# Loads on two queues, half-partition decay loads and a new hand-written order in a fused linear-attention and long-convolution kernel

## The chip, the cores and the metric

The kernel runs on one core of one Trainium2 chip. Its time is the device time in microseconds (us) of one execution. Three runs of the kernel before gave a median of 153.95 us, from 152.64 to 155.37.

The core has engines that run their own instruction streams in order and meet through semaphores: PE (TensorE, matrix products into the banks of PSUM), DVE (VectorE), ACT (ScalarE), POOL (GpSimd) and SP (SyncE). Transfers between DRAM and the on-chip memory are issued by an instruction on the queue of some engine and carried out by 16 DMA engines.

## The reference

Two stages follow one another. The first is a recurrence over 768 positions for 4 batches and 8 heads of width 48 (`state` is 48 x 48 per head); the second is a gated long convolution over the 384 channels that the first gives:

```python
for t in range(S):                       # S = 768
    cur = einsum('bhd,bhe->bhde', u * k[t], v[t])
    y[t] = einsum('bhd,bhde->bhe', r[t], state + cur)
    state = w[t] * state + einsum('bhd,bhe->bhde', k[t], v[t])
x = y.transpose(0, 2, 1, 3).reshape(B, S, 384)
x1, x2, x3 = split(x @ w_proj, 3)        # w_proj: 384 x 1152
conv = irfft(rfft(x2, axis=1) * rfft(filter_fft, axis=0))
out = (x1 * conv * x3) @ w_out
```

r, k, v and w are float32 of shape 4 x 8 x 768 x 48; the output is 4 x 768 x 384 float32.

## The kernel before

**Chunks.** Each batch is cut into 6 chunks of 128 positions, 24 chunks in all. Chunk i needs four loads, `lw{i}`, `lk{i}`, `lr{i}`, `lv{i}`, each 128 positions x 8 heads x 48 float32 = 192 KB. A head's row of one position is 48 x 4 = 192 bytes, and it is the longest run that is contiguous on both sides. Chunks 0 and 1 form groups of their own; the others go in pairs, so there are 13 groups `gi`, and some operations (`ln`, `vb`, `rk`, `ru`, `rh`, `cc`, `vc`) treat a whole group.

**First stage, for one chunk.** `ln` (ACT, line 1319) takes the logarithm of w. `cs` (PE, lines 1345 to 1350) forms running sums of it over the 128 positions by two products with triangular masks, and four products with a column of ones for the total. `ex` (ACT, 1353) is the exponential of the sums in place in PSUM. `kq` (DVE, 1356) multiplies it with k and r. `ph` (ACT, 1360) gives the chunk's total decay. `tr` (PE, 1368) transposes kq in eight 128 x 128 blocks into a bank, and `qk` (DVE or ACT) copies the bank out. `sc` (PE, 1380) is the score product, `mt` copies it out with its causal mask on DVE (`D` one half, `M` both), or copies it plainly on ACT (`A`, `N`) and `mc` on POOL cuts the triangle. `kv` and `ki` (PE) form the next state, `su` (DVE, 1431) scales it. `rk`, `ru`, `rh` and `cc` give the weight of the term with u, `vc` multiplies it with v, and `xa`, `yi` or the addition in `xn` brings it into the result. `ys` and `y` (PE, 1450 and 1458) form the output, `xn` evicts it, `yt` (PE, 1482) transposes it and `xT` copies it out of the bank as the input of the second stage.

**Second stage, for one batch b.** `p`/`cp` is the projection x1 and its eviction, `q`/`cq` (DVE, 1649) x3 times x1, `xw`/`cxw` the projection x2, `sd` sums and differences of its two halves, `f`/`cf` the forward transform, `u` and `p{b}.{n}` on DVE the product with the filter's spectrum, `E`/`cE`/`aE` (and `dE` for the folded form, letter `Q`) the inverse transform, `yE` the gate, `o`/`co`/`so` the output projection, its eviction and the store. The second stage of batch b runs between the chunks of batch b+1; that of batch 3 stands alone at the end.

**What sets the order.** A string, `ORDER`, names every operation, the engine that does it, the PSUM bank where it takes one, and sometimes an operation that it must follow. A line reads for example `cs0 P 4`, `kq0 D`, `lw0 S` or `rh0 G kq0`. Each engine works through its own lines in the order of the string; `-` means that the operation is left out because another form does it. Semaphores for the data are added by the framework. `warm n b` puts n products of 256 columns of zeros on PE. All 96 loads, the load of u and of the filter and all 13 stores are on SP's queue; the four weight loads are on POOL's.

**Buffers.** There are 3 slots for w (`NLW`), 4 for k and r and for v (`NLD`), each holding a pair of chunks; 3 groups of the products (`NG`); 4 of `kq` and `qk` (`NF`); 5 output slots (`NO`), taken in turn by `co`. An instruction that fills a slot waits for the last reader of it.

Of the kernel before, what the change touches and what calls it, by code (L numbers as in the profile page):

```python
# [9 lines left out]
FP32 = mybir.dt.float32  # L10
# [28 lines left out]
NLW, NLD, NG, NF, NS, NX, NO = 3, 4, 3, 4, 3, 3, 5  # L39
# [5 lines left out]
warm 16 0  # L45
pads D
smalls D
zeros D
lw0 S
first A  # L50
ln0 A
imaps G
maske G smalls
maps G smalls
ang2 D
ang1 D
lw3 S
lw2 S
lr0 S
lk0 S  # L60
kz2 G
maskn G
cs0 P 4
kz0 G
ln2 A
u S
signs D
maski G
ia1.0 G
ex0 A  # L70
kq0 D
ia2.0 D
warm 9 1
cs3 P 6
kz3 G zeros
cs2 P 2
ur A
warm 5 1
um P 0
rk0 G  # L80
ub A
lv0 S
lw1 S
lr3 S
lk1 S
tr0 P 1
qk0 D
ph0 A
vb0 A
ex3 A  # L90
ln1 A
ang0 D
ru0 G ia2.0
rh0 G kq0
cc0 D
kz1 D
vc0 D
warm 6 0
sc0 P 0
warm 2 4  # L100
cs1 P 4
mt0.1 -
mt0.0 N
kv0 P 0
ex2 A
ex1 A
ia0.0 G zeros
su0 D
mc0.0 C cc0
lk3 S  # L110
lr1 S
mc0.1 -
warm 4 1
yi0 P 0
kq3 D
y0 P
xn0 A
tr3 P 1
kq1 D
lk2 S  # L120
lr2 S
lv1 S
lw4 S
lw5 S
tr1 P 0
rk1 G
ru1 D
rh1 G ru1
ph1 A
qk3 D  # L130
xa0 -
ph3 A
kq2 D
lv2 S
lv3 S
yt0 P 6
sc3 P 4
xT0 A
mt3.0 M
qk1 A  # L140
vb1 A
ph2 A
warm 4 7
tr2 P 6
lr4 S
lk4 S
ki1 P 1
sc1 P 2
qk2 A
mc3.0 -  # L150
mt1.1 -
kv1 P
warm 2 7
sc2 P 6
cc1 D
rk2 G
lk5 S
ru2 D
ia2.1 G
vc1 G  # L160
mc1.1 -
mt1.0 M
mc1.0 -
mt2.1 -
mt3.1 -
lr5 S
ln3 A
warm 5 0
cs4 P 4
yi1 P 2  # L170
rh2 G ru2
su1 D
vb2 G ru2
ys1 P
mc2.1 -
lv5 S
lv4 S
cc2 D
vc2 G cc2
mt2.0 M  # L180
wproj1 G mt2.0
ki2 P 0
y1 P
lw6 S
warm 5 1
kv2 P
xn1 A
ex4 A
cs5 P 2
xa1 -  # L190
mc2.0 -
yt1 P 1
su2 D
ki3 P 0
kv3 P
# [3 lines left out]
mc3.1 -  # L199
xT1 A  # L200
kq4 D
tr4 P 1
ex5 A
ph4 A
wproj0 G su2
kq5 D
su3 D
xn2 A
yi3 P 4
ys3 P  # L210
qk4 A
y3 P
rk3 G
xn3 D
warm 4 6
tr5 P 6
qk5 D
xa2 -
ph5 A
yt2 P 2  # L220
lw7 S
xa3 -
yt3 P 7
xT3 D
xT2 D
ki4 P 5
warm 4 1
sc5 P 6
trig A
sin0 A  # L230
sin2 A
vb3 G xn3
mt5.1 -
mc5.1 -
ia1.1 G xT2
kv4 P
sc4 P 3
ia0.1 G xT2
mt4.0 N
ru3 D  # L240
rh3 D
cc3 D
vc3 G cc3
warm 7 1
xw0.2 P 0
is A
mt5.0 M
su4 D
mt4.1 -
xw0.0 P 2  # L250
mc5.0 -
mc4.0 C
yi5 P 6
cxw0.2 D
yi4 P 4
cxw0.0 D
lk7 S
sin1 A
table A
ln4 A  # L260
lr7 S
mc4.1 -
ys5 P
ys4 P
y5 P
xn5 D
y4 P
xn4 D
p0.0.0 P 0
lk6 S  # L270
xa4 -
xa5 -
yt5 P 6
p0.2.0 P 3
lr6 S
rk4 G xn5
xT5 D
yt4 P 2
cs7 P 6
cp0.0.0 D  # L280
filt S
cp0.2.0 D
cs6 P 4
xT4 A
xw0.4 P 0
ex7 A
kq7 D
lv7 S
ex6 A
kq6 D  # L290
cxw0.4 A
if3 A
p0.0.1 P 2
tr7 P 1
ph7 A
cp0.0.1 A
tr6 P 6
qk6 A
qk7 A
sd0.0.0 D  # L300
ru4 D
lw8 S
lw9 S
p0.2.1 P 0
ph6 A
warm 4 7
f0.0 P 2
lv6 S
cp0.2.1 A
cf0.0 A  # L310
sd0.1.0 D
f0.2 P 5
sc7 P 0
mt7.1 -
rh4 D
fsd0 D
fsd1 D
lk8 S
lr9 S
cf0.2 A  # L320
warm 5 7
sc6 P 6
lr8 S
mt7.0 N
mt6.1 -
warm 6 4
h1 P 1
mt6.0 M
ln5 A
cc4 D  # L330
h2 P 4
mc6.0 -
mc7.1 -
lk9 S
mc7.0 C rh4
hc1 A
hg1 D
vb4 G
vc4 G fsd1
lv8 S  # L340
lv9 S
mc6.1 -
lk11 S
hc2 A
h0 P 6
hg2 D
kv6 P 3
su6 D
lk10 S
lw10 S  # L350
lr10 S
hc0 A
cs8 P 0
wproj2 G
warm 2 2
yi6 P 4
y6 P
lw11 S
hg0 D
ex8 A  # L360
xn6 A
xa6 -
yi7 P 2
ys7 P
y7 P
xn7 A
xa7 -
cs9 P 4
kq8 D
lr11 S  # L370
ex9 A
yt6 P 3
yt7 P 7
xT7 D
kq9 D
xT6 A
ki7 P 2
kv7 P
tr8 P 6
qk8 D  # L380
ph8 A
rk5 G cc4
ru5 G
vb5 A
lv11 S
xw1.0 P 0
lr12 S
lv10 S
tr9 P 3
sc8 P 6  # L390
if2 A
ph9 A
lw12 S
rh5 D
cc5 D
lk12 S
lw13 S
lv13 S
cxw1.0 A
qk9 A  # L400
lv12 S
mt8.1 -
su7 D
lk13 S
mt8.0 M
vc5 G cc5
lk15 S
f0.1 P 4
q0.2.0 P 3
ki8 P 2  # L410
cq0.2.0 D
mc8.1 -
sc9 P 0
lr13 S
cf0.1 A
mt9.0 N
mc9.0 C
if1 A
kv8 P
q0.0.1 P 6  # L420
q0.2.1 P 3
yi8 P 4
ln6 A
u10.0 D
mt9.1 -
su8 D
cq0.0.1 D
mc8.0 -
u00.0 D
yi9 P 1  # L430
lw15 S
ys9 P
ys8 P
y8 P
lk14 S
mc9.1 -
xn8 A
lw14 S
lr14 S
xa8 -  # L440
y9 P
lr15 S
q0.0.0 P 6
lv15 S
yt8 P 0
cs10 P 4
if0 A
xn9 A
xa9 -
ki9 P 2  # L450
yt9 P 1
lk17 S
cq0.0.0 D
lv14 S
xT8 A
ex10 A
xT9 A
kv9 P
lw17 S
cs11 P 6  # L460
ex11 A
p1.2.0 P 0
cq0.2.1 D
rk6 G cq0.0.1
cp1.2.0 A
su9 D
lv17 S
ru6 D
xw1.2 P 1
kq10 D  # L470
tr10 P 3
kq11 D
rh6 G ru6
ph10 A
cxw1.2 A
p1.0.0 P 4
cc6 D
p0.0 D
ph11 A
qk10 A  # L480
cp1.0.0 A
ln7 A
tr11 P 7
vb6 G
vc6 G
q1.0.0 P 1
qk11 D
sc10 P 3
sc11 P 6
q1.2.0 P 5  # L490
lr17 S
lw16 S
ki10 P 0
mt10.1 A
cq1.0.0 D
cs12 P 1
mt10.0 D
lk16 S
yi10 - 3
ys10 P  # L500
mt11.1 -
mc11.1 -
mc10.0 -
mc10.1 G
y10 P
mt11.0 N
cs13 P 6
kv10 P
cq1.2.0 D
ex12 A  # L510
xn10 V
kq12 D
vb7 G
ex13 A
E0.0 P 4
mc11.0 C mt10.0
ph12 A
yi11 - 1
cE0.0 A
su10 D  # L520
kq13 D
ph13 A
tr12 P 3
ys11 P
kv12 P 0
aE0.0.0 D
rk7 G
ru7 G
xa10 -
qk12 A  # L530
y11 P
E0.1 P 6
xn11 V
xa11 -
su12 D
cE0.1 A
aE0.0.1 D
dE0.0.0 -
rh7 G aE0.0.0
yt11 P 1  # L540
xT11 D
yt10 P 0
ki13 P 3
tr13 P 2
E0.2 P 4
kv13 P
aE0.1.1 D
aE0.1.0 D
xT10 A
qk13 D  # L550
ln8 A
cE0.2 A
sc12 P 6
lk18 S
lr16 S
mt12.1 -
su13 D
aE0.2.1 D
aE0.2.0 D
mt12.0 N  # L560
sc13 P 0
p1.0.1 P 2
mt13.1 D
mt13.0 D
lv16 S
cp1.0.1 A
cs14 P 6
ex14 A
dE0.1.0 -
xw1.4 P 4  # L570
q1.0.1 P 1
cc7 D
kq14 D
cq1.0.1 D
p1.2.1 P 3
vb8 A
cxw1.4 A
rk8 G
ru8 G
rh8 G aE0.1.0  # L580
tr14 P 0
ph14 A
mc12.1 -
cp1.2.1 A
dE0.1.1 -
sd1.1.0 D
q1.2.1 P 5
cs15 P 3
ki14 P 2
kv14 P  # L590
qk14 A
ex15 A
vc7 G sd1.1.0
sd1.0.0 D
sc14 P 6
mt14.0 A
ln9 A
su14 D
mt14.1 D
mc14.1 -  # L600
f1.0 P 0
lw18 S
f1.2 P 6
cf1.0 A
dE0.0.1 -
kq15 D
cq1.2.1 D
ph15 A
dE0.2.1 -
mc12.0 C cq1.0.1  # L610
cf1.2 A
tr15 P 2
cc8 D
cs16 P 0
yi12 - 4
y12 P
yE0.0 D
vc8 G
qk15 D
mc13.1 -  # L620
f1.1 P 6
yi13 P 2
xn12 V
sc15 P 4
xa12 -
ex16 A
kq16 D
mc13.0 -
ys13 P
y13 P  # L630
cf1.1 A
ph16 A
tr16 P 7
mt15.1 D
vb9 A
cs17 P 0
xn13 A
lw19 S
mt15.0 D
mc14.0 G yE0.0  # L640
ex17 A
qk16 D
yE0.1 G
lk19 S
ki15 P 6
kv15 P
yi14 - 3
ys14 P
lr18 S
lv18 S  # L650
yt12 P 5
xa13 -
su15 D
yt13 P 2
xT12 A
y14 P
xn14 X
mc15.1 -
ki16 P 7
kv16 P  # L660
sc16 P 5
lv19 S
lr19 S
ln10 A
rk9 G mt15.1
xT13 D
kq17 D
mc15.0 -
ph17 A
mt16.1 A  # L670
dE0.2.0 -
xa14 G
xw2.0 P 3
mt16.0 D
yi15 P 0
ys15 P
y15 P
su16 D
cxw2.0 A
u11.0 D  # L680
cs18 P 6
yt14 P 2
xn15 A
xT14 D
ex18 A
xa15 -
lr20 S
lw21 S
cs19 P 4
ex19 A  # L690
tr17 P 3
yt15 P 0
wout G su16
xT15 A
kq18 D
rk10 G
ph18 A
kq19 D
ru9 D
qk17 A  # L700
lw20 S
ph19 A
p2.0.0 P 1
tr18 P 0
ru10 D
xw2.2 P 6
mc16.0 -
q2.0.0 P 4
rh9 D
rh10 D  # L710
cp2.0.0 A
cxw2.2 A
lk20 S
yE0.2 D
tr19 P 2
cq2.0.0 D
sc17 P 6
vb10 G rh10
p2.2.0 P 1
cc9 D  # L720
mt17.1 -
o0.0 P 4
mt17.0 M
qk18 A
cc10 D
qk19 A
mc17.1 -
lk21 S
q2.2.0 P 0
lr21 S  # L730
cp2.2.0 A
ln11 A
kv18 P 3
co0.0 A
mc16.1 G
cq2.2.0 D
sc18 P 1
mt18.1 D
# [1140 lines left out]
```

## Time and profile before

| what | value |
|---|---|
| median of 3 runs | 153.95 us (152.64 to 155.37) |
| the profiled execution's own time | 153.79 us |
| its span, first to last instruction | 152.1 us |
| busy: PE, DVE, ACT, POOL | 142.4, 135.6, 123.1, 96.1 us |
| instructions: PE, DVE, ACT, POOL | 1725, 252, 204, 101 |
| moved by DMA | 26.23 MB in 104118 packets, 100129 of them under 512 bytes |
| loads: issue to landing, median | 3.8 to 4.4 us |

The span is 1.69 us below the time of the same execution; what lies around the span is not seen in the profile. "Idle" of an engine is time in which none of its instructions runs; the view of waits says what ended it. Neighbouring instructions of DVE and ACT overlap a little, so that the mean durations of all 252 DVE instructions add up to about 151.3 us against 135.6 us busy, which is 0.062 us of overlap for each. Instructions that issue DMAs are not counted as busy; they stand as `SPq` on SP's queue.

### The profile page before, as it was taken

How to read it: one execution, taken by the hardware profiler on the slowest of the kernel's cores; microseconds unless marked ns; L12 is line 12 of the kernel's file. 1: busy time of each engine (PE TensorE's matmuls, PEld its weight loads, DVE VectorE, ACT ScalarE, POOL GpSimd, SP SyncE). 2: the span in 40 equal slices, each digit the busy share in tenths (PEclk: the TensorE clock that was granted, in tenths of full speed). 3: DMA queues.
4: the chain of work that ended last, by engine and by line, in shares of the span. 5: the costliest groups of instructions: out<-in, count | busy, mean ns of one | idle time of the engine just before them, and what ended most of it. 6: DMA issues, size and time to landing. Idle time of an engine off the chain costs nothing.

```text
span 152.1 us, 4409 instructions
## 1 busy us (share of the span) xinstructions
PE 142.4 (94%) x1725; PEld 95.3 (63%) x1725; DVE 135.6 (89%) x252; ACT 123.1 (81%) x204; POOL 96.1 (63%) x101
## 2 busy tenths in 40 slices
PE   7986999999999999999999999999999999999980
PEld 5654667666556657567666776576687666656530
DVE  3589996989969999999989999999999999999950
ACT  4576849989979989997889899979999987576370
POOL 6577989944069567888968974885299164830310
PEclk9999999999999999999999999999999999999999
DMA  4999899999999999989899899998940000002956
GB/s 97 216 214 223 163 221 174 203 182 272 250 209 170 197 172 219 212 162 218 170 203 218 160 203 192 198 213 169 324 133 0 4 0 0 4 0 88 395 210 240
DMA packets 104118, 26.23 MB, mean 172 GB/s; under 512 B 100129, under 2 KB 102690, under 8 KB 104098
## 3 DMA queue, kind: packets, MB, share of 16 engines
q1 hardware_dynamic: 102498, 24.78, 74.2%
q0 software_dynamic: 1600, 1.18, 5.6%
q8 instruction: 13, 0.21, 0.5%
q14 instruction: 7, 0.06, 0.1%
HBM read 22.41 MB, written 4.72 MB: 178 GB/s over the span
## 4 chain that ended last, share of the span: by engine, by line
PE 42%; DVE 15%; DMA 13%; SPq 10%; ACT 8%; issue 5%; POOL 4%; POOLq 1%; DVEq 0%; ACTq 0%
SPq L1313 10%; PE banks L1624 7%; PE banks L1511 6%; PE banks L1780 5%; DMA w<-in_w_dram 5%; PE banks L1661 3%; PE banks L1368 3%; PE banks L1380 3%; DMA v<-in_v_dram 3%; DMA kr<-in_r_dram 3%; DVE kq L1356 3%; PE banks L1458 3%; DMA kr<-in_k_dram 2%; ACT banks L1353 2%; PE banks L1716 2%
## 5 line engine op out<-in xcount | busy, mean ns | idle before, releaser
L1209 POOL TENSOR_TENSOR rk<-kr 128x768 bf16<-128x768 f32 (+1 forms) x13 | 23.0, 1766 | 9.5 <-DMA kr<-in_r_dram 5.9
L1624 PE MATMUL banks<-xT,wproj 128*128 128x384 bf16 x144 | 27.9, 326 | 0.2 <-ACT x L1213 0.2
L1356 DVE TENSOR_TENSOR kq<-banks,kr 128x768 bf16<-128x768 f32 x24 | 22.4, 949 | 3.6 <-DMA kr<-in_k_dram 1.7
L1401 POOL TENSOR_SCALAR_AFFINE_SELECT mt<-mt 128x512 bf16<-128x512 bf16 (+1 forms) x15 | 14.0, 940 | 12.7 <-ACT mt L1213 8.6
L1209 POOL TENSOR_TENSOR vc<-vb,cc 128x768 bf16<-128x768 bf16 (+1 forms) x11 | 17.4, 1577 | 5.1 <-DVE cc L1332 3.3
L1353 ACT ACTIVATE banks<-banks 128x768 f32<-128x768 f32 x24 | 19.1, 806 | 0.5 <-PE banks L1350 0.2
L1624 PEld LDWEIGHTS <-wproj 128*128 128x128 bf16 x144 | 13.0, 97 | 8.1 <-issue 0.7
L1213 ACT ACTIVATE x<-banks 128x768 bf16<-128x768 f32 (+1 forms) x24 | 16.8, 709 | 1.6 <-PE banks L1661 1.1
L1396 DVE TENSOR_TENSOR mt<-banks,mask_excl 128x1024 bf16<-128x1024 f32 (+1 forms) x17 | 16.2, 965 | 0.2 <-PE banks L1380 0.2
L1213 ACT ACTIVATE qk<-banks 128x1024 bf16<-128x1024 bf16 x16 | 16.2, 1029 | 0.0
L1368 PE MATMUL banks<-ident,kq 128*128 128x128 bf16 x192 | 14.3, 219 | 1.4 <-ACT xn L1213 0.6
L1259 PE MATMUL banks<-wt 128*128 128x256 bf16 x90 | 14.4, 300 | 1.1 <-DVE wt L1282 1.1
L1368 PEld LDWEIGHTS <-kq 128*128 128x128 bf16 x192 | 11.8, 97 | 4.2 <-DVE kq L1356 1.6
L1780 PE MATMUL banks<-wout,y 128*128 128x384 bf16 x72 | 13.3, 326 | 0.5 <-DVE g L1649 0.3
L1661 PE MATMUL banks<-wproj,xT 128*128 128x384 bf16 x72 | 13.6, 325 | 0.0
L1511 PE MATMUL banks<-sd,F 128*128 128x384 bf16 (+1 forms) x96 | 13.4, 328 | 0.2 <-ACT phi L1360 0.2
L1319 ACT ACTIVATE lg<-w 128x768 bf16<-128x768 f32 (+1 forms) x13 | 10.4, 799 | 3.4 <-DMA w<-in_w_dram 3.4
L1213 ACT ACTIVATE mt<-banks 128x512 bf16<-128x512 f32 (+1 forms) x15 | 11.6, 802 | 1.1 <-PE banks L1380 0.7
L1213 ACT ACTIVATE o<-banks 128x768 f32<-128x768 f32 (+1 forms) x12 | 9.3, 785 | 3.5 <-PE banks L1780 3.4
L1511 PEld LDWEIGHTS <-F 128*128 128x128 bf16 (+1 forms) x120 | 8.5, 103 | 5.8 <-issue 1.1
L1649 DVE TENSOR_TENSOR g<-banks,x 128x384 bf16<-128x384 f32 (+1 forms) x16 | 11.8, 748 | 0.3 <-PE banks L1624 0.2
L1209 DVE TENSOR_TENSOR U<-X,hh 128x2304 bf16<-128x2304 bf16 (+1 forms) x12 | 11.9, 1022 | 0.0
(109 smaller groups left out, 331.1 us busy)
## 6 DMA issues: line engine op xcount, KB each, us to landing
w<-in_w_dram SPq DMA_DIRECT2D x24, 192.0 KB, 4.4
kr<-in_r_dram SPq DMA_DIRECT2D x24, 192.0 KB, 3.9
kr<-in_k_dram SPq DMA_DIRECT2D x24, 192.0 KB, 3.8
v<-in_v_dram SPq DMA_DIRECT2D x24, 192.0 KB, 3.9
out_dram<-o SPq DMA_DIRECT2D x11, 384.0 KB, 4.0
U<-in_moe_filter_fft_dram SPq DMA_DIRECT2D x1, 1152.0 KB, 7.3
wproj<-in_moe_w_proj_dram POOLq DMA_DIRECT2D x3, 288.0 KB, 5.9
out_dram<-o SPq DMA_DIRECT2D x2, 192.0 KB, 2.2
```

Source lines behind the costliest of these rows:

```text
L1209: return eng(e).tensor_mul(o, a, b)
L1213: return nc.scalar.activation(out=o, in_=a, func=AF.Copy)
L1259: nc.tensor.matmul(banks[:, at, 0:256], wt[:, 0:L], wt, start=True, stop=True)
L1313: op(f"l{name}{i}", [SP], lambda e, bk, t=t, x=x, q=q, rw=rw: nc.sync.dma_start(out=t[:, q], in_=x[b, :, rw, :].rearrange("h t d -> t h d" ...
L1353: op(f"ex{i}", [ACT], lambda e, bk: nc.scalar.activation(out=two(bk, f"cs{i}")[:, :, 0:C], in_=two(bk, f"cs{i}")[:, :, 0:C], func=AF.Exp), ...
L1356: op(f"kq{i}", [DVE], lambda e, bk: nc.vector.tensor_mul(kq[f][:, :, :, 0:D], two(bk, f"cs{i}")[:, :, 0:C].rearrange("p a (h d) -> p a h d ...
L1368: nc.tensor.transpose(p[:, HP * m + j, :], kq[f][:, m, 2 * j:2 * j + 2, :], ident)
L1396: return copy(ACT, o, x) if e in (ACT, ACT2) else nc.vector.tensor_mul(o, x, _mid(mask_excl, z - HP * a))
L1511: nc.tensor.matmul(p[rows], F[:, ti, c0 + rows.start:c0 + rows.stop], x[q][:, ti, :], start=(ti == 0), stop=(ti == NT - 1),)
L1624: nc.tensor.matmul(p, wproj[:, cb, col0:col0 + L], xT[bx][:, cb, sl], start=(cb == 0), stop=(cb == CB - 1),)
L1661: nc.tensor.matmul(view(bk)[:, z], xT[bx][:, cb, (c0 + z) * L:(c0 + z + 1) * L], wproj[:, cb, C:2 * C], start=(cb == 0), stop=(cb == CB - 1),)
L1780: nc.tensor.matmul(view(bk)[:, z], yt_[:, z, :], wout[:, cb, :], start=(cb == 0), stop=(cb == CB - 1),)
```

## The change

What it does:

- 24 of the 96 loads are issued by ACT instead of SP: `lw3 lw0 lr0 lk3 lr1 lr2 lv2 lw5 lk4 lw7 lv6 lk8 lw8 lw10 lk11 lv12 lv11 lw15 lr14 lw14 lw18 lr16 lv16 lv22`, in this order among ACT's own work.
- For groups 2 to 5 (chunks 2 to 9) w is loaded into 64 partitions with two neighbouring positions in each, so that the contiguous run is 384 bytes. `cs` of these chunks takes two products with half the rows for each one before (four of 384 columns, eight of one column), with masks `mask_two` made at the start.
- `ORDER` is written anew. Engines of single operations change with it: on DVE 13 instructions more in all, on ACT 15 fewer, on POOL 2 more. Of `mt`, DVE has 16 half and 7 whole ones (8 and 9 before), ACT 5 whole ones (7 before).
- `qk` of chunks 18 to 23 and `xT` of the same chunks become DMA transposes on SP's queue; `tr` and `yt` of these chunks fall away on PE, and the copies out of the bank with them (4 of `qk` on ACT, 2 on DVE, and 7 fewer of `xT` on ACT, one more on DVE).
- `E3` takes the folded form (`Q`), which adds six `dE3` (two on POOL); `E1.1` takes the plain form, and two `dE1` fall away.
- Three gates go through ACT and POOL (`xq`, `gq`) instead of `cq` on DVE.
- The output slots go from 5 to 4. The `xf` buffer keeps one slot, of which u takes a part; two `xe` buffers are new.
- `warm` makes products of up to 512 columns; 83 units of 256 columns instead of 90, of which 17 have 124 columns. Other new forms (`ew`, `kw`, `aw`) are left out by the order (`-`).

The diff, cut to its core:

```diff
-NLW, NLD, NG, NF, NS, NX, NO = 3, 4, 3, 4, 3, 3, 5
+NLW, NLD, NG, NF, NS, NX, NO = 3, 4, 3, 4, 3, 3, 4
+PAIRS = range(2, 6)
+HL = L // 2
+NTURN = 8
...
+    def folded(t):
+        return t.rearrange("p a h d -> p (a h d)").rearrange("p (h x) -> p h x", h=H)
+    def ring(e):
+        return nc.scalar if e == ACT else nc.sync
...
+            if gi in PAIRS:
+                op(f"lw{i}", [SP, ACT], lambda e, bk, q=q, rw=rw: ring(e).dma_start(
+                    out=folded(wl[sw])[q * HL:q * HL + HL],
+                    in_=w[b, :, rw, :].rearrange("h (p e) d -> p h (e d)", e=2)), ...)
...
-                op(f"l{name}{i}", [SP], lambda e, bk, t=t, x=x, q=q, rw=rw: nc.sync.dma_start(
+                op(f"l{name}{i}", [SP, ACT], lambda e, bk, t=t, x=x, q=q, rw=rw: ring(e).dma_start(
...
+        def cs_halves(e, bk):
+            p = two(bk, f"cs{i}")
+            at = slice(q * HL, q * HL + HL)
+            for z, m in ((0, "n"), (1, "e")):
+                for par in (0, 1):
+                    nc.tensor.matmul(
+                        p[:, z, 0:C], mask_two[m][at, par, :], lg[fg][at, par, :, 0:D], start=not par, stop=bool(par),
+                    )
+            for j in range(HP):
+                for par in (0, 1):
+                    nc.tensor.matmul(
+                        p[:, 1, C + j:C + j + 1], lg[fg][at, par, 2 * j:2 * j + 2, :], ones[at],
+                        start=not par, stop=bool(par),
+                    )
...
+        def turn_qk(e, bk):
+            if e == SP:
+                return nc.sync.dma_start_transpose(out=qk[f], in_=kq[f].rearrange("p a h d -> p (a h d)"))
+            return copy(e, qk[f].rearrange("p a t -> p (a t)"), one(bk, f"tr{i}").bitcast(BF16))
...
+        def turn_x(e, bk):
+            if e == SP:
+                return nc.sync.dma_start_transpose(out=xT[b % 2][:, :, rows], in_=xn[:, i % NX])
+            return copy(e, xT[b % 2][:, :, rows], turned(bk))
...
+            op("x" + n3, [WIDE, NONE], lambda e, bk: copy(ACT, x3, view(bk, n3)), ...)
+            op("g" + n3, [POOL, NONE], lambda e, bk: nc.gpsimd.tensor_mul(g[bx][:, fs, sl], x3, x1[:, fs, sl]), ...)
```

Of the new order, the stretch with the last loads and the transposes on SP's queue, and the end of the chunks (lines of other engines between them left out where "..." stands):

```diff
+kq20 D
...
+qk20 S
+lk22 S
+lr22 S
...
+lr23 S
+lv23 S
+lk23 S
+kq23 D
+qk21 S
...
+lv22 A
+qk22 S
+sc21 P 6
...
+qk23 S
+xT18 S
+xT19 S
...
+so0.1 S
+xT20 S
+so0.0 S
+xT21 S
+xT23 S
...
+xT22 S
+so0.2 S
+so1.1 S
```

## The prediction

> **What bounds the kernel now.** I read the page's first two parts, then busy time by stretch, then what DVE and ACT waited for, and last the transfers and SP's queue.
>
> ```profile
> span 152.1 us, 4409 instructions
> PE 142.4 (94%) x1725; PEld 95.3 (63%) x1725; DVE 135.6 (89%) x252; ACT 123.1 (81%) x204; POOL 96.1 (63%) x101
> ...
> DVE  3589996989969999999989999999999999999950
> ...
> DMA  4999899999999999989899899998940000002956
> ```
>
> The slices say where each limit lies: the DMA engines are full from slice 2 to slice 28 (108 us), DVE from slice 8 (27 us) to slice 37 (144 us). By stretch:
>
> ```profile
> 0.00:30.00 30.00, 26.12 (x334) 18.49 (x335) 22.98 (x63) 21.05 (x35) 24.15 (x43) 1.00 1.01 189
> 30.00:80.00 50.00, 49.00 (x615) 32.46 (x612) 46.80 (x74) 44.98 (x73) 33.16 (x25) 1.00 1.00 203
> 80.00:140.00 60.00, 59.68 (x740) 40.16 (x735) 59.12 (x103) 52.32 (x91) 36.96 (x33) 1.00 0.55 116
> ```
>
> Columns: stretch, length, busy PE, PEld, DVE, ACT, POOL, clock, DMA share, GB/s. From 80 to 140 us PE (59.7 of 60) and DVE (59.1) are both full, so taking work from PE alone buys nothing there. ACT is idle for 80 - 21.05 - 44.98 = 14.0 us before 80 us and little else. What DVE waited for:
>
> ```profile
> DVE o L1215 <- ACT o L1213: 1.7, 1, 1.7
> DVE kq L1356 <- DMA kr<-in_k_dram: 1.7, 1, 1.7
> DVE o L1496 <- POOL o L1238: 1.4, 1, 1.4
> DVE kq L1356 <- DMA kr<-in_r_dram: 1.3, 1, 1.3
> DVE hh L1586 <- ACT hh L1585: 0.9, 1, 0.9
> ```
>
> DVE's idle is 152.1 - 135.6 = 16.5 us. 4.0 lie before the first kq at 7.68 us (0.9 at the start, 1.4, and the 1.7 for k), 5.4 at the end (the 1.7 for ACT, then 152.1 - 148.4 for the last store), 7.1 between. Of these 7.1 only 1.3 are a wait for a load. So **DVE is the bound**, and the full DMA engines reach it mostly through the order that was made around them.
>
> **DVE's work.** I went through both orders and gave every operation the mean of its row. Added: eight half masks at 0.68 (+5.5), four `dE` at 0.35 (+1.4), three `yE` (+1.3), two `xn` with addition at 0.55 (+1.1), `ur` and `ub` at 0.55 (+1.1). Removed: two whole masks at 1.22 (-2.4), three `cq` (-2.0), two `qk` at 0.68 (-1.4), two `ru` at 0.63 (-1.3). The small rest gives +0.3. Sum +3.6 us in 13 more instructions; less the overlap of 0.062 each, **+2.7 us busy**. It lies on the engine that is full from 27 us on, so it counts, except for what falls into idle time: by the order 7.4 us of DVE work now stand before and in the first kq instead of 5.3, which takes about 1.5 of the 4.0 us of idle there.
>
> **Loads.** Between 50 and 60 us SP's queue moved 9305 packets in 91.9% of 16 x 10 us:
>
> ```profile
> q1 hardware_dynamic: 9305, 1.76, 91.9%
> ```
>
> That is 15.8 ns for a piece of 192 bytes, 1.01 us for a load of 1024. No row has pieces of 384 bytes. Bounds: 15.8 ns (only the count matters) and 31.6 (only the bytes). The stores, 3072 bytes in a piece at 393 GB/s, take 125 ns each; the line through both points gives 23 ns, so 0.74 us for 512 pieces. I take that: 0.27 saved on each of 8 loads, 2.2 us of the engines' time up to chunk 9, with bounds 0 and 4.0. DVE sees of it the one wait for a load, 1.3 us, which I let go; what is late next is PE and ACT, which feed DVE.
>
> **ACT.** Its own work shrinks by 10.1 us of means (four `qk` at 1.03, seven `xT` at 0.50, two whole masks at 1.02), 9.1 busy, but only 5.6 of it before the place of kq15 at 81 us, and 23 of its 24 loads stand before that place. What an issue costs ACT no row shows. SP's rows (shortest, median and longest issue in ns):
>
> ```profile
> L1313 SPq DMA_DIRECT2D w<-in_w_dram x24: 423/826/3935, 0.8 to 100.6; - x24
> L1313 SPq DMA_DIRECT2D kr<-in_r_dram x24: 553/898/3077, 2.6 to 104.2; - x24
> ```
>
> SP's first three issues in the chain that ended last (start, duration):
>
> ```profile
> 0.79 0.42 SPq L1313
> ...
> 1.27 0.58 SPq L1313
> ...
> 1.90 0.64 SPq L1313
> ```
>
> Into empty queues an issue takes 0.42 to 0.64; the medians of 0.83 to 0.90 are those of a queue that always holds some four loads (3.9 us to landing at 1.01 each). ACT's own queue seldom holds more than one, so I take 0.5: 23 x 0.5 = 11.5 less 5.6 is 5.9 us, against 14.0 idle less some 4 that come before the first w lands. It fits. But behind each issue wait `ln`, `ex`, `qk` and the evictions, in order, and PE and DVE wait for those: 1.0 us, with bounds 0 and the first rival.
>
> **PE.** `cs` of eight chunks gains two products of 384 columns (0.16 each by the chain) and four of one column (0.08): 0.4 each, +3.2 us between 15 and 65 us. The warm products fall from 90 to 74 units of 0.13: -2.1. Late, six `tr` (0.45) and six `yt` (0.17) fall away, -3.7, and the folded `E3` saves about 1.0. The early extra is covered by warm products, which only fill gaps; the late gain is worth nothing while DVE is full.
>
> **DMA transposes.** None is in the trace. The nearest rows are transfers of 192 to 384 KB: stores land after 1.9 to 4.3 us, loads after 2.7 to 8.1. The way through PE costs 0.45 + 0.68 to 1.03. So `qk` comes 0 to 3 us later; but in the trace kq22 ends at 110.8 and its scores run at 116.5, kq23 at 113.2 and 119.7: six us of cover. `xT23` has less: the eviction ends at 126.1, its projection starts at 129.1, 3 us. Queued behind the transposes on SP are the loads of chunks 22 and 23 (behind qk20, which waits for kq20) and the first two stores. In the new order some 11 us of DVE work lie between kq20 and kq23, and qk20 with five loads and a landing needs about 2 + 5 + 2. Taken: 0.5 us, bounds 0 and 6 (twelve times 0.5 not covered).
>
> **Output slots.** With four, `co1.1` waits for the store so0.0 to land, and `co3.1`, near the end, for so2.0, which is issued only about 2.5 us before. Stores of the tail land after 1.9 to 4.3: 0 to 1.8 us. Taken: 0.5. Behind `co1.1` wait ACT's evictions of the last projections, but ACT has its 9 us of relief there. The POOL's sum is unchanged (94.3 both).
>
> **Sum against the span:** 152.1 + 2.7 (DVE) - 1.5 (idle at the start) - 1.3 (wait for a load) + 1.0 (ACT's issues) + 0.5 (transposes) + 0.5 (slots) = 154.0. The profiled execution took 1.69 us beyond its span, 153.79 against a median of 153.95, so no correction: **155.7 us**. With the bounds of these terms the case reaches from 152.5 to 158.5.
>
> **Rivals.**
>
> *ACT becomes the bound (slower).* The point that decides: (10 + 5.6) / 23 = 0.68 us for an issue, between the 0.42 to 0.64 of an empty queue and the 0.83 to 0.90 of a full one. [...] Against: the first three. At 0.85, 19.6 - 5.6 - 10 = 4 us over, and with 1 us for the rest and part of DVE's extra 158.5 to 160; at 1.2, 12 us over, 166. [...] Chance 0.27, time 160.
>
> *The transposes on SP's queue are slow (slower).* If each holds the queue for 3 us or more, lk23 comes after its place, and the tail's xT23 is 2 to 3 us late. Price 3 to 6 us: 159. Chance 0.08.
>
> *The gaps close (faster).* If loads are 4.0 us shorter and the new order fills the start (-2.5) and 4 of the 7.1 us between: 152.1 + 2.7 - 2.5 - 4.0 = 148.3, 150.0 us. For: 24 early loads leave SP, so that r0 and k0 are issued side by side. Against: the first kq still needs five loads at 1.01 us through the same engines, and only 1.3 us of the gaps are a load's. Chance 0.21.
>
> *The shorter w loads are not shorter.* Then 2.2 us fewer come early, 157 at most: inside the forecast's range.
>
> **Chances.** Forecast 0.44. Within 2% of 153.95 is 150.9 to 157.0, about what a measurement of this kernel can tell from no change. The forecast has 0.33 inside and 0.11 above; the fast case 0.17 below and 0.04 inside; the slow ones 0.34 above and 0.01 inside. Faster 0.17, same 0.38, slower 0.45. The range reaches from the fast case's 150 into the first rival, to 163.
>
> **What would show it.** DVE busy near 138.3 us, its idle near 15.5, of which 2.5 before the first kq; ACT's issues near 0.5 us each; the w loads of chunks 2 to 9 with 512 packets and about three quarters of the engine time; DVE still full from 80 to 140 us, with PE below 58 of 60. ACT issues above 0.7 us, or DVE waiting for ACT between 20 and 80 us, would make the forecast wrong upwards; DVE idle below 11 us downwards.

## The result and the profile after

The changed kernel takes **162.21 us** (median of 4 runs, 160.91 to 163.82) against 153.75 us, a ratio of 1.0547 with a 95% interval of 1.0439 to 1.0655: slower. The profiled execution took 162.31 us with a span of 160.6, so 8.5 us of span more than before. The forecast was 155.7 us, the range 150 to 163. (Ratios here leave out executions that a slower state of the chip lengthened, so they can differ from the quotient of two medians.)

First two parts of the page of the changed kernel (engine busy times; tenths in 40 slices of 4.0 us):

```profile
span 160.6 us, 4304 instructions
PE 143.6 (89%) x1670; PEld 91.3 (57%) x1670; DVE 139.6 (87%) x266; ACT 114.8 (71%) x189; POOL 95.8 (60%) x103
...
DVE  6475479999899853999999999999999999999970
...
PEclk9956779999999999999999999999999999999997
DMA  4999999979999899999458999199999652704265
```

DVE now has two dents, in slices 3 to 5 and in slices 14 and 15; from slice 16 (64 us) on it is full as before. Over the first dent stands something that the page of before had nowhere: TensorE's granted clock is not 9 but 5 to 7. The same stretches as in the prediction, for the changed kernel (length, busy PE, PEld, DVE, ACT, POOL, clock, DMA share, GB/s):

```profile
0.00:30.00 30.00, 24.91 (x270) 14.77 (x271) 21.05 (x60) 15.94 (x27) 19.98 (x42) 0.83 1.18 198
30.00:80.00 50.00, 44.78 (x564) 29.69 (x563) 44.47 (x69) 37.43 (x61) 28.72 (x24) 1.00 1.06 196
80.00:140.00 60.00, 58.95 (x751) 38.78 (x750) 58.64 (x101) 50.84 (x87) 42.40 (x35) 1.00 0.83 164
```

After 80 us nothing is amiss. The whole loss lies before. The start of each chunk's `kq` on DVE dates it (us from the start of the span; the last row is the span):

| | before | changed | later by |
|---|---|---|---|
| kq0 | 7.68 | 8.70 | 1.0 |
| kq2 | 15.69 | 19.46 | 3.8 |
| kq4 | 22.08 | 28.27 | 6.2 |
| kq6 | 36.42 | 41.21 | 4.8 |
| kq8 | 49.13 | 54.21 | 5.1 |
| kq10 | 60.69 | 71.34 | 10.7 |
| kq12 | 67.62 | 78.24 | 10.6 |
| kq20 | 100.99 | 109.89 | 8.9 |
| end | 152.08 | 160.60 | 8.5 |

Two losses of some 5 us each, at 8 to 28 us (**A**) and at 54 to 71 us (**B**), and 2.1 us won back from kq12 to the end (82.4 us against 84.5).

**Loss A.** The stretches around the first dent in the changed kernel (columns as above), and what PE's products waited for longest in the whole span (total, times, longest):

```profile
4.00:8.00 4.00, 2.61 (x16) 1.00 (x15) 1.96 (x6) 2.10 (x4) 1.86 (x6) 1.00 1.40 218
8.00:15.00 7.00, 6.48 (x50) 3.55 (x49) 4.43 (x10) 3.18 (x6) 4.74 (x12) 0.51 1.41 218
15.00:18.00 3.00, 1.27 (x25) 1.12 (x25) 1.95 (x3) 0.30 (x1) 1.18 (x3) 1.00 1.38 217
18.00:22.00 4.00, 4.00 (x42) 2.98 (x41) 2.03 (x4) 3.00 (x6) 2.10 (x2) 0.57 1.35 216
```

```profile
PE banks L1379 <- DVE kq L1327: 2.3, 1, 2.3
PE banks L1560 <- ACT phi L1534: 2.1, 1, 2.1
PE banks L1560 <- ACT x L1331: 2.0, 1, 2.0
PE banks L1495 <- ACT lg L1466: 1.4, 1, 1.4
```

The fourth line is a gap of 1.39 us at 4.97 to 6.36 us, in which PE waits for the first Ln; the first w (`lw0`), now the second load on ACT's queue and beside SP's loads, lands at 5.8 us instead of 3.5. The second and third lines belong to loss B. The first line is a gap of 2.25 us at 14.48 to 16.73: the *warm products* themselves (L1379) wait for kq1, since they are written into columns 388 and up of a bank that kq1 still reads. Behind the two gaps PE runs at half clock, in 8.1 to 14.9 and in 18.3 to 21.7 us. In the clock's record these are 6.83 and 3.41 us, 10.2 in all, three pieces of 3.41. In the second window PE is "busy" for 6.48 of 7.00 us, but at half clock, and DVE behind it stands idle for 2.6. (The clock's record begins only at 4.7 us here and at 5.4 before. Up to there a warm product of 512 columns takes 0.43 us here and later 0.22, and one of 256 columns 0.21 us before and later 0.11, so both kernels start at half clock, though the page's row shows a 9 there.)

The length of a gap alone does not tell what follows it here: behind gaps of 1.39 and 2.25 us the clock was halved, while PE's gaps of 2.12 us (at 57.35) and 1.97 us (at 61.40) in loss B left it whole. How much PE did around each of them stands in the last section.

**Loss B.** From the chain that ended last of the changed kernel (start, duration, what):

```profile
54.21 0.79 DVE kq L1327
55.00 6.97 DMA kr<-in_r_dram
61.97 0.02 issue
61.99 0.46 ACTq L1460
62.45 0.05 issue
62.50 0.82 ACT x L1331
63.32 0.04 issue
63.36 0.40 PE banks L1560 x8
```

Nobody needs lr12, the load of 6.97 us, at 62 us. But ACT's *issue* of another load, lv11, waits for its landing, and behind that issue stand ACT's evictions, and behind these PE's scores. Why one load waits for another shows when the trace's issues are set in order by semaphore. SP's and ACT's queues share eight (100, 102, 104 to 109), and each issue below lists that semaphore among what it waits for (the one of lv12 in the semaphore instruction just ahead of it). Six loads on ACT were issued right behind the landing of the last DMA on their semaphore:

| load on ACT | issued | the last on its semaphore, landed |
|---|---|---|
| lk3 | 4.06 | lw3 (ACT), 4.04 |
| lr1 | 8.14 | lr0 (ACT), 8.12 |
| lr2 | 10.28 | lr3 (SP), 10.26 |
| lw5 | 15.72 | lv1 (SP), 15.70 |
| lv12 | 58.83 | lv10 (SP), 58.75 |
| lv11 | 61.99 | lr12 (SP), 61.97 |

Each follows within 0.1 us, and of the 100 issues in this trace for which that landing can be told none comes ahead of it. In the kernel before no issue came sooner than 2.48 us after the landing of the last DMA on its semaphore: at most four other loads were under way when one was issued, all from one queue. With two queues it is up to six, and the order in which they are issued is no longer that in which the semaphores were given out. ACT stood still 0.39, 1.77, 1.47, 3.12 and 2.07 us before the last five of these. An *issue* itself is cheap; the changed kernel's issues by line (shortest, median, longest in ns):

```profile
L1460 ACTq DMA_DIRECT2D v<-in_v_dram x6: 374/406/463, 13.4 to 121.1; - x6
L1460 ACTq DMA_DIRECT2D kr<-in_r_dram x5: 374/374/621, 2.2 to 80.4; - x5
L1454 ACTq DMA_DIRECT2D w<-in_w_dram x4: 602/615/702, 0.8 to 41.6; - x4
```

### The profile page after: what moved, and what is told of

The parts are those of the page before. It is cut to its first block, busy times and chain, and to the rows that moved or that the text cites. A ratio compares the mean times of both kernels' runs of the same rounds, so it can differ in the third digit from the quotient of the medians.

```text
span 160.6 us, 4304 instructions
## 1 busy us (share of the span) xinstructions
PE 143.6 (89%) x1670; PEld 91.3 (57%) x1670; DVE 139.6 (87%) x266; ACT 114.8 (71%) x189; POOL 95.8 (60%) x103
## 4 chain that ended last, share of the span: by engine, by line
PE 60%; DVE 19%; DMA 10%; issue 3%; ACT 2%; POOL 2%; ACTq 1%; POOLq 1%; DVEq 0%; SPq 0%
PE banks L1809 11%; PE banks L1696 7%; PE banks L1542 5%; PE banks L1989 5%; PE banks L1906 5%; PE banks L1379 4%; DMA kr<-in_r_dram 4%; PE banks L1850 4%; DVE mt L1576 3%; PE banks L1560 3%; PE banks L1638 3%; DMA v<-in_v_dram 3%; PE banks L1505 3%; DVE kq L1327 3%; DMA w<-in_w_dram 3%
## 5 line engine op out<-in xcount | busy, mean ns | idle before, releaser
L1576 DVE TENSOR_TENSOR mt<-banks,mask_excl 128x512 bf16<-128x512 f32 (+1 forms) x23 | 19.0, 844 | 4.3 <-PE banks L1560 4.2
L1327 POOL TENSOR_TENSOR rk<-kr 128x768 bf16<-128x768 f32 (+1 forms) x12 | 21.0, 1747 | 1.5 <-DVE U L1327 1.5
L1331 ACT ACTIVATE x<-banks 128x768 bf16<-128x768 f32 (+1 forms) x26 | 18.0, 708 | 5.0 <-DMA kr<-in_r_dram 2.6
L1581 POOL TENSOR_SCALAR_AFFINE_SELECT mt<-mt 128x512 bf16<-128x512 bf16 (+1 forms) x13 | 12.2, 939 | 9.7 <-ACT mt L1331 6.0
L1379 PE MATMUL banks<-wt 128*128 128x512 bf16 (+2 forms) x53 | 13.5, 388 | 3.4 <-DVE kq L1327 2.3
L1331 ACT ACTIVATE qk<-banks 128x1024 bf16<-128x1024 bf16 x12 | 12.3, 1027 | 5.1 <-PE banks L1542 5.0
L1333 POOL CAST vb<-v 128x768 bf16<-128x768 f32 (+1 forms) x8 | 6.3, 782 | 12.4 <-DVE P L1765 9.7
L1477 POOL TENSOR_TENSOR rk<-rk 128x384 bf16<-128x384 bf16 (+1 forms) x8 | 8.0, 997 | 9.5 <-DVE rk L1327 6.3
L1560 PE MATMUL banks<-qk 48*128 48x128 bf16 x192 | 9.3, 225 | 4.1 <-ACT phi L1534 2.1
L1542 PE MATMUL banks<-ident,kq 128*128 128x128 bf16 x144 | 11.8, 230 | 0.0
```

The lines of the kernel that those rows point to most:

```text
L1327: return eng(e).tensor_mul(o, a, b)
L1331: return nc.scalar.activation(out=o, in_=a, func=AF.Copy)
L1379: nc.tensor.matmul(banks[:, at, lo:hi], wt[:, 0:L], x, start=True, stop=True)
L1542: nc.tensor.transpose(p[:, HP * m + j, :], kq[f][:, m, 2 * j:2 * j + 2, :], ident)
L1560: nc.tensor.matmul(p[:, par, j, :], qk[f][p0:p0 + D, j, :], qk[f][p0:p0 + D, HP + j, :], start=True, stop=True,)
L1576: return copy(ACT, o, x) if e in (ACT, ACT2) else nc.vector.tensor_mul(o, x, _mid(mask_excl, z - HP * a))
```

## The experiments

Theory W: ACT is held by loads that wait for another landing. Theory C: a gap of PE costs half clock. Against both stand the prediction's rivals (the issue's own cost; slow DMA transposes) and the thought that the DMA engines, full until 70 us, set the pace whatever one does. The edits of the order are shown as lines of it; "A" is ACT, "S" is SP.

### Two of ACT's loads on SP

```
-lv12 A
+lv12 S
-lv11 A
+lv11 S
```

> The changed kernel with two of its 24 ACT loads, lv12 and lv11, issued by SP at the same places of the order. In the changed kernel ACT stands still for 3.12 us in front of the issue of lv12 (58.83) and for 2.07 us in front of lv11 (61.99), each time until the load eight before it has landed. Theory W (ACT's in-order queue is held by a load that waits for the load eight before it): the loss of some 5 us between 54 and 71 us goes, 157 to 158.5 us, kq10 starts near 66 instead of 71.3, ACT has no stop of over 1 us between 55 and 65. Theory C (all of the loss comes from PE's clock at the start): within 1 us of the changed kernel, 161 to 163. Theory I (an issue costs ACT too much): 2 of 24 issues, under 1 us, 161.5.

Measured: 160.06 us (158.68 to 162.14), 1.0297 [1.0187, 1.0406], span 158.5. From kq8 to kq10 it takes 11.6 us, as before (11.6), not 17.1: loss B is gone, and no issue on ACT is held there. But kq8 comes at 56.6, 2.4 later than in the changed kernel, and that is a third gap of PE, with its half clock:

```profile
38.00:42.00 4.00, 2.94 (x56) 2.10 (x55) 3.86 (x7) 1.81 (x3) 1.00 (x1) 1.00 1.29 253
42.00:46.00 4.00, 4.00 (x30) 2.40 (x29) 3.10 (x6) 2.33 (x5) 0.00 (x0) 0.57 1.19 212
```

PE stood 1.06 us at 39 us (chunk 6's products wait for a bank), as it had in the changed kernel at 38.1 *without* the clock being lowered. So theory W holds for this stretch, but its total does not: 2.1 instead of 4 to 5 us shorter, since the gap, moved by 0.9 us, was now followed by half clock.

### More warm products at the start

```
 um P 2
+warm 14 5
-warm 6 0 388
+warm 12 7
-warm 11 0 388
+warm 6 5
```

> The changed kernel with more warm products at the start, nothing else: a new group of 14 products after the products on P, which wait for nothing new, 12 products that no longer wait for kq1 in place of 6 that do, and 6 that wait for nothing in place of 11 that wait for kq1. No load and no issue is moved. Theory C (PE stood idle in 4.97 to 6.36 and 14.48 to 16.73 us, the granted clock fell to 0.5 in 8.07 to 14.90 and 18.31 to 21.72, and DVE then waited for PE): the clock is 1.0 from some 3 us on, kq4 starts near 23 to 24 instead of 28.3, and 157 to 158.5 us. Theory W (the issues on ACT alone): clock better, time within 1 us of the changed kernel, 161 to 163, since ACT is late anyway.

Measured: 162.68 us (160.17 to 164.0), 1.0397 [1.0285, 1.0509], span 162.3. From 6.2 us on the clock stays whole up to 43 us, and kq4 comes at 25.8 instead of 28.3, kq6 at 37.8 instead of 41.2. All of it is then lost: lw8 waits on ACT until another load lands at 41.07 (PE idle for 2.2 us, half clock at 43.8 to 47.2, and once more between 64 and 68), and lv12 and lv11 are issued at 58.71 and 62.28, as in the changed kernel at 58.83 and 61.99, because the loads that they wait for land when they did there; kq10 comes at 71.7. Theory C's mechanism is shown, its price is not: in this execution, at 164.0 us the longest of the four, ACT's held issues swallow what the start wins; the shortest took 160.17.

### All loads on SP, without and with the warm products

Every `A` behind one of the 24 loads becomes `S`; the second kernel has the warm products of the run above as well.

> The changed kernel with all 24 ACT loads on SP at the same places of the order; the rest of the change (two tokens a partition in w, the new order, the DMA transposes, four output slots) stays. Theory W: the loss between 54 and 71 us goes whole and the first w lands as early as before, 154 to 158 us; what is left over the kernel before is the clock at the start. Theory C: the first w lands earlier, so part of PE's gap at 5 us goes, but the gap at 14.5 us stays: 158 to 161. Theory S (SP's one queue is the narrower place, which is why the loads were split): loads of the first 20 us come late, SP's issues at 0.8 us each, 162 to 166 us.

> Both edits together: all loads on SP, and the additional warm products at the start. If the two losses (clock at the start, ACT held by waiting loads) are separate and are all there is: 150 to 154 us, at or below the kernel before, with kq4 near 22 to 24 and kq10 near 61 to 64. If one hides the other: no better than the better one alone, 156 to 159. Theory S (SP's queue is the narrower place): 160 or more.

Measured: 161.3 us (160.56 to 161.91), 1.0425 [1.0352, 1.0498], and 162.45 us (160.9 to 163.62), 1.0468 [1.0369, 1.0567]; spans 160.2 and 159.2. The first lies just above theory C's forecast and far from W's, the second far from what separate losses would give and within what theory S gave. In the first, kq8 to kq10 is 12.7 us, so loss B is mostly gone, but the half clock of the start lasts to 14.0 us, the gap at 14.9 us stays, and one of 1.41 us at 39 us is followed by 6.8 us of half clock:

```profile
41.00:48.00 7.00, 7.00 (x52) 4.56 (x51) 5.04 (x10) 3.04 (x6) 0.00 (x0) 0.52 0.97 185
```

In the second, PE's waits between 20 and 40 us begin with

```profile
PE banks L1622 <- DVE kq L1328: 5.5, 1, 5.5
```

since lk4, at the end of SP's queue, is issued at 22.8 us and lands only at 30.4 (in the first of the two at 22.7 and 26.7; why it took 7.6 us here isn't shown). In the next kernel, where it stays on ACT, it is issued at 17.8. So the split of the loads does do something: it lets a single load past the queue. These two kernels made me doubt theories W and C and let the DMA engines in as a rival: four kernels with different starts had all come to kq10 at 71.1 to 71.7 us.

### All gaps in one

Seven loads on SP (lr1, lr2, lw5, lk8, lw8, lv11, lv12), the warm products of the second run, and

```
+warm 8 2
 cs6 P 6
```

> The changed kernel with the gaps of the first four runs closed in one: the warm products of the second run at the start, seven ACT loads whose issue held ACT (lr1, lr2, lw5, lk8, lw8, lv11, lv12) on SP at the same places, and a group of 8 warm products before the products of chunk 6, where PE stood idle for 1.0 to 1.4 us near 39 us in four of the kernels (38.13 in the changed one) and three of them fell to half clock from 42 us on. The other 17 loads stay on ACT. Theory G (any idle of PE over about 1 us costs some microseconds of half clock, ACT's held issues cost their own length, and nothing else is slower than before): granted clock 1.0 up to 70 us, kq10 near 62 to 64, 152 to 156 us. Theory D (the loads themselves are late, since the DMA engines are full up to 70 us, and every gain at the start is waited away later, as the second and fourth run came to kq10 at 71.7 and 71.1 like the changed kernel's 71.3): kq10 again at 70 to 72, 160 to 162.

Measured: 156.56 us (155.57 to 157.82), 1.0165 [1.0089, 1.0241], span 153.8, clock whole from 7.1 us on, kq10 at 63.2. Theory G has the clock and kq10 right and the time 0.6 us too low; the DMA engines are out as the cause, since over the first 70 us they are as full as in the changed kernel (1.11 against 1.13). In this kernel the additional products ahead of cs6 write into the bank that still holds the y of chunk 5, so that chunk's batch isn't the reference's; the later runs have them in a free bank. One held issue was left, lw18, 1.79 us, with PE idle for 1.34 us at 73.3.

### Each part of the change alone, in the old order

These are the kernel before with one part each: DMA transposes for chunks 18 to 23 (`tr18 - 0`, `qk18 S`, `yt18 - 5`, `xT18 S` and so on), w of chunks 2 to 9 as 64 partitions with two tokens each, and the 24 loads on ACT. The rest of the change (the new order itself, the engines of single operations, the folded `E3`, four output slots) has no run of its own.

> The kernel before, its own order, with one part of the change: qk and xT of chunks 18 to 23 transposed by DMA on SP at the places where the evictions stood, and the PE transposes of these chunks gone. From kq12 to the end the changed kernel takes 82.4 us and the kernel before 84.5. If the transposes earn these 2.1 us: 151 to 153. If the new order or the four output slots earn them: 153.5 to 155. If a DMA transpose comes later than PE and the eviction (3.7 us to landing for qk, 2.3 for xT) and DVE or PE then wait, since the old order leaves it no room: 156 to 160.

> The kernel before, its own order, all loads on SP, with one part of the change: w of chunks 2 to 9 as 64 partitions with two tokens each, the four half masks on POOL behind the old masks, and the split products. (A scratch tile has two slots instead of three, so that it fits; it is used twice.) Cost alone: PE 8 x 0.4 more, POOL four masks more at the start, the loads' share less by 8 x 0.27 us. If PE's additional products lie in its idle time and the loads gain: 152.5 to 154. If the masks or the products come late for the first chunks: 155 to 157. If it opens a gap of PE that lowers the clock: 157 to 160.

> The kernel before, its own order, with one part of the change: the same 24 loads issued by ACT, at their old places. Theory W (each load waits for the landing of the load eight before it, which holds up nobody on SP but everything behind it on ACT): ACT stands still for several microseconds in all in front of single issues, and the time is 156 to 162. Theory I (an issue costs ACT its 0.4 us and no more): 24 x 0.38 = 9 us of ACT in 14 us of idle, 153 to 155.5.

| part alone | time, us | ratio | span | kq10 | kq20 |
|---|---|---|---|---|---|
| DMA transposes | 163.37 (162.54 to 163.52) | 1.0588 [1.0522, 1.0654] | 161.7 | 61.3 | 102.1 |
| w in pairs | 155.62 (155.45 to 155.91) | 1.0102 [1.0056, 1.0147] | 153.8 | 63.8 | 102.8 |
| 24 loads on ACT | 173.95 (173.36 to 174.98) | 1.1296 [1.1229, 1.1364] | 172.1 | 79.6 | 120.5 |

**The transposes** lose 9.6 us of span (the expectation of a later run says 7.8, which is wrong), all but 1.1 of it after kq20. PE's waits in that kernel between 90 and 130 us begin with the scores (L1387), which wait for a transpose:

```profile
PE banks L1387 <- DMA qk<-kq: 5.5, 3, 4.0
```

They land 3.2 to 5.3 us after the issue, median 4.4, and the issue itself stands in SP's queue behind loads (kq20 ends at 103.1 us, its transpose is issued at 109.8); the old order leaves them the room of a transpose on PE and its eviction. Behind PE's longest stop there, 4.05 us at 110.0, the clock is halved once more, from 113.9 to 117.3.

**The pairs** cost 3.1 us by kq10 (63.82 against 60.69) and 1.8 at the end. 3.1 is as much as the 8 x 0.4 us of PE that the prediction had covered by warm products. Clock and gaps are as before.

**The loads on ACT** are by far the dearest: ACT is held, PE waits up to 4.95 us at a time, and the clock falls (mean 0.939). From its chain:

```profile
59.90 5.04 DMA v<-in_v_dram
64.94 0.02 issue
64.96 0.38 ACTq L1316
65.33 0.05 issue
65.38 0.61 ACT mx L1563
```

Again an ACT issue follows the landing of a load that it has nothing to do with (lv10, for lv11) by 0.02 us; ACT had been held for 4.4 us. Theory W, beyond its own forecast.

### Gaps closed, without pairs, and with late chunks turned on PE

The first kernel is that with all gaps closed, its products in front of chunk 6 in bank 3, lw18 on SP, and

```
+lw0 S
+lw3 S
-lw3 A
-lw0 A
```

The second is the first with `PAIRS = range(0)` and without the half masks; the third is the first with `tr`, `qk`, `yt` and `xT` of chunks 18 to 23 on PE and ACT at the places of the DMA transposes.

> The kernel of the run with the closed gaps, with its extra warm products in front of chunk 6 in a free bank, and two edits more: lw18, in front of whose issue ACT stood 1.79 us there (PE idle 73.29 to 74.63), on SP, and the very first loads in the old kernel's order (lw0, then lw3, both on SP, so that the first w need not share the DMA engines with lw3 and lw2). Theory G (gaps of PE and held issues are what the loads on ACT cost, each to be had back on its own): about 1.3 us less after 73 us and up to 1 us less at the start than that run's span of 153.8, so 153 to 155.5 us, granted clock 1.0. Theory D (what is gained at the start is waited away later, since the DMA engines are full): kq10 again at 63, 155 to 156.5.

> The kernel of the run above, with w of all chunks again as 128 partitions with one token each: the half masks and their zeroing, and the split products gone, everything else as there. In the old order that part alone moved kq10 by 3.1 us (60.69 to 63.82) and the end by 1.8. Theory P (PE's 8 x 0.4 us of additional products are not covered by warm products but come whole): kq10 some 2 to 3 us earlier than in the run above, the end 1 to 2.5 us: 151 to 153.5, below the kernel before. Theory L (the shorter loads pay for them: 8 x 0.27 us of full DMA engines): the same time as the run above within 0.7, or longer, 154 to 156.

> The kernel of the first run of this call, with qk and xT of chunks 18 to 23 turned on PE and evicted by ACT again, at the places where the DMA transposes stand. PE gets 6 x 0.45 + 6 x 0.17 = 3.7 us and ACT 6 x 1.03 + 6 x 0.50 = 9.2 us more after 100 us. In the old order the DMA transposes cost 7.8 us (161.7 against 152.1 of span, 1.8 of it by the time that kq20 to kq22 wait). If the new order covers them and their relief of PE and ACT counts: 1 to 4 us longer than that first run, 155 to 158. If DVE is full there in any case, so that the relief is worth nothing: within 0.7 of it. If they still cost something in the new order: 1 to 3 us shorter, 150.5 to 153.

Measured: 155.3 us (12 runs, 153.53 to 156.85), 1.0056 [1.0008, 1.0105]; 157.67 us (6 runs, 155.08 to 159.41), 1.0235 [1.0172, 1.0298]; 167.84 us (6 runs, 165.62 to 169.66), 1.081 [1.0741, 1.0879].

The first has the time that theory G gave. In its profiled execution (156.67 us) the first loads in the old order are no gain: kq0 comes at 10.8 us instead of 9.0. The chain leads there through `u`, which PE's second group of products needs and which now comes later, and then through 3.0 us of warm products at half clock, which lasts to 9.3 us in this execution.

Without pairs, kq10 comes at 60.9 us, as in the kernel before (60.7), so the 2 to 3 us of PE are there in this order too. Theory P still fails: its 151 to 153.5 us lie below all six runs. Whether the kernel is longer than with the pairs is less sure, since its times spread over 4.3 us and the shortest, 155.08, lies within the range of the first kernel. Its trace is that of this shortest run: from kq10 to kq20 it takes 40.9 us, with the pairs 38.6, and from kq20 to the end 51.6 against 50.2, where PE waits for a late transpose,

```profile
PE banks L1832 <- DMA xT<-xn: 1.0, 1, 1.0
```

which landed 3.8 and 4.3 us after their issue in two cases, where 2.3 is the median of the changed kernel. Why its other runs take up to 4 us more than the profiled one stays open.

The third tells little. Its transposes stand on PE, in order, right behind kq, where a DMA could wait on SP's queue without holding anybody, and some of them write into a bank that still holds another late chunk's y, so that the output of the last batch isn't the reference's. What it shows is that this order has no place for them as it stands (span 167.8, of which 4.4 us of loss by kq20 and 8.4 behind it). What the transposes are worth where each has its own best place wasn't tried.

### Only the gaps closed

The changed kernel with eight loads on SP (lw18 too), the warm products, those in front of chunk 6 in bank 3, and its first loads as it had them:

```
-lr1 A, lr2 A, lw5 A, lk8 A, lw8 A, lv12 A, lv11 A, lw18 A
+the same, S
+warm 14 5          (behind um P 2)
-warm 6 0 388
+warm 12 7
-warm 11 0 388
+warm 6 5
+warm 8 3           (ahead of cs6 P 6)
```

> The changed kernel with only its gaps closed and its first loads as it had them (lw3 and lw0 on ACT): the eight ACT loads that held ACT in one of the runs (lr1, lr2, lw5, lk8, lw8, lv11, lv12, lw18) on SP at the same places, 16 loads left on ACT, and the additional warm products at the start and in front of chunk 6 (in a free bank). Theory G: the span of the first run with closed gaps (153.8) less the 1.3 us of PE's stop at 73.3 us, so 152.0 to 153.0, and 153.5 to 155 us of time; kq0 again at 9.0 and kq4 at 25.1, where the run that put lw0 first on SP had 10.8 and 26.9. If putting lw0 first was no loss and the span of 155.0 there is this order's own: 155 to 156.5.

Measured: 155.32 us (12 runs, 153.8 to 160.06), 1.0067 [1.0021, 1.0113]. The profiled execution took 153.8 us; the head of its page and the stretches:

```profile
span 152.1 us, 4316 instructions
PE 142.3 (94%) x1673; PEld 90.1 (59%) x1673; DVE 135.8 (89%) x266; ACT 114.4 (75%) x189; POOL 95.6 (63%) x103
...
PEclk9999999999999999999999999999999999999999
```

```profile
0.00:30.00 30.00, 26.74 (x305) 15.71 (x305) 23.67 (x67) 19.13 (x31) 23.18 (x44) 1.00 1.14 196
30.00:80.00 50.00, 49.22 (x620) 32.56 (x619) 46.13 (x76) 40.39 (x67) 33.20 (x28) 1.00 1.07 208
```

152.1 us is the span of the kernel before, to 0.1 us. PE is busy for 76.0 of the first 80 us instead of 69.7, DVE for 69.8 instead of 65.5. kq4 comes at 24.2, kq10 at 63.5, kq20 at 102.5. This execution is the shortest of the twelve; by the ratios 0.7% is left of the 5.5%. So nearly all of the changed kernel's loss is held issues, gaps and what follows from them. That putting lw0 first costs time isn't shown, though: kq0 comes at 8.6 us here and at 10.8 there, but the ratios of the two kernels agree within their intervals.

This kernel, with the first of the section above the best of the study, doesn't beat the one before: it is 0.2 to 1.1% longer.

## Why the prediction was right or wrong, point by point

The sign and the range held; the forecast itself was 6.5 us short. That the range held is luck: by the bounds of its own terms the case reached only to 158.5, and the range went on to 163 to take in the first rival. The time of 162.2 lies near that rival's 160, and yet not by the price of an issue on ACT. Of the signs that were to show it wrong upwards, one came: between 20 and 80 us DVE waited 4.1 us for ACT, against 1.5 before. The other, issues on ACT above 0.7 us, did not: their median is 0.38, the longest took 0.70.

- **"The early extra is covered by warm products, which only fill gaps"** is the step that failed first. In this kernel the warm products also keep the clock whole: with more of them, in the second run, it was 1.0 from 6.2 to 43 us. The changed order had fewer of them, and two groups of them waited for kq1. 10.2 us of half clock followed, loss A. And the extra was not covered either: the pairs alone cost 3.1 us by kq10.
- **ACT: "behind each issue wait `ln`, `ex`, `qk` and the evictions ... 1.0 us"** is the second. The issue's price was even lower than the 0.5 taken (median 0.38 us, 10.9 us for 24, 6.5 of them beside a running activation), and the mean of 0.46 stayed well under the point that decides, 0.68 (the longest one took 0.70). What was missed is that an issue can be held: five were, for some 8.8 us in all, by landings on a shared semaphore. The trace of before could have warned only by the number of semaphores, eight, beside four loads under way; no issue waited there.
- **First rival (ACT becomes the bound).** For its 160 it needed issues of 0.85 us on ACT. They are short there (median 0.38 us), although 8.6 of their 10.9 us lie inside an issue of SP. SP's did grow: their medians by row of the profile are 0.79 to 0.93 us against 0.75 to 0.90 (the prediction showed two of the four rows), their mean 1.19 against 1.01; why isn't shown. The number came out, for another reason.
- **Shorter w loads.** 23 ns for a piece of 384 bytes was right for the median, 22, and low for the mean, 28.0. A load of 512 pieces is thus 0.70 to 0.90 us. The case without pairs was no faster, though kq10 came earlier, so something pays for the pairs in this order; whether it is the shorter loads, and how much they are worth, isn't settled.
- **DVE +2.7.** The instructions came to 14 more (13 forecast), busy to 139.6 us (138.3 forecast). But with the gaps closed the same 266 instructions are busy for 135.8, as long as the 252 before. Single ones differ between the two traces (one `mx` 1.53 and 0.32 us, one product of the spectrum 2.70 and 1.35); a mean of a row was too coarse for a term of this size.
- **Start, -1.5.** DVE's idle before the first kq fell from 4.42 us (4.0 in the prediction) to 3.57, but that kq came 1.0 us later.
- **DMA transposes, +0.5; four slots, +0.5.** In the new order neither shows as a wait of DVE after 80 us beyond 1.0, and the changed kernel is 2.1 us *shorter* from kq12 on. That the cover was the order's, and no property of the transposes, is shown by their 9.6 us in the old order.
- **The sum.** Against the kernel with closed gaps the forecast of the rest, 154.0 of span, stands at 152.1; by its runs +0.7% [0.2, 1.1] of time where +1.1% was forecast. So the sum of the terms that I wrote down nearly holds, but not term by term: DVE's +2.7 came to +0.2 there, and the first kq came 0.9 us later instead of earlier. That they cancel is luck. The loss lay in two terms that I set at nothing and at 1.0.

## What to carry to other kernels

Before a load moves to an engine that computes, look up which DMA last used its semaphore and when that lands: here an issue cost ACT 0.38 us in the median, ACT was held up to 4.4 us in front of one (the 24 loads on ACT in the old order), and everything behind it in the engine's order pays. Products that only keep TensorE warm can be part of the critical path (4% of the chain that ended last in the changed kernel, L1379); count them and their waits as such, and look at the granted clock before anything else when a kernel gets slower by some per cent. The length of a single gap tells little there: in the changed kernel one of 1.39 us stood before half clock and one of 2.12 us did not. Parts of a change that were ordered together can each be a loss in the old order (1%, 6% and 13% here), so a part tried alone says what its place is worth, not what the part is.

## What the runs showed of the hardware

- The length of a gap did not tell whether TensorE's clock was halved. In the changed kernel gaps of 1.39 and 2.25 us stood before half clock, gaps of 1.06, 2.12 and 1.97 us did not; with two of ACT's loads on SP one of 1.06 us did, with all loads on SP one of 1.41 us did too, and in the first kernel with all gaps closed one of 1.34 us did not.
- In the changed kernel's trace the record of the clock begins at 4.66 us and changes at 8.07, 14.90, 18.31, 21.72 and 158.26 us; these points lie 1, 2, 1, 1 and 40 times 3.41 us apart. Before, it begins at 5.42 us and changes at 152.19, just behind the end of the span and 43 times 3.41 us later. Cut from its beginning into pieces of 3.41 us, the two records give 87 pieces inside the spans. The following was worked out from them afterwards, and no run was made to test it. For each piece, add up the columns of PE's products, each spread over its time in the trace and weighted by the share of 128 rows and 128 columns that the profile's row shows (a product marked `48*128` counts 0.375), and divide by what 3.41 us hold at whole clock, 2.4 columns per ns (384 columns in 0.16 us).

| the piece's clock | the next piece's clock | pieces | their sums |
|---|---|---|---|
| whole | half | 3 | 0.26, 0.345, 0.366 |
| whole | whole | 81 | 0.375 to 0.985 |
| half | half | 1 | 0.31 |
| half | whole | 2 | 0.376, 0.47 |

- By these sums the gaps of the changed kernel fall into place. Loss A's two lie wholly or mostly in pieces of 0.366 and 0.345, loss B's in pieces of 0.39 and 0.375; the gap of 1.06 us is divided between pieces of 0.67 and 0.46. In the kernel before, where the clock stayed whole, the lowest piece has 0.45 (from 12.24 us). Three pieces ahead of half clock are few; whether such sums tell anything elsewhere isn't shown.
- In the changed kernel eight DMA semaphores served both queues, and six loads on ACT were issued 0.02 to 0.08 us after the last DMA on their semaphore had landed; no issue came ahead of such a landing.
- A DMA transpose of qk (128 x 1024 bf16, 256 KB) took 3.2 to 4.0 us to land in the changed kernel and 3.2 to 5.3 alone in the old order, and its issue took 1.2 to 2.2 and 1.3 to 3.0 us of SP; the smaller one of xT landed after 2.3 us in the median in both, and after 3.8 and 4.3 in two cases without pairs.
